# Eight PSUM banks in one pool by stage, second layers behind their twelve Strassen units, two rings of weight loads, and low parts on VectorE

## The chip, the cores and the metric

One core of a Trainium2 chip runs one program. It has five engines with a queue each: TensorE (PE, with weight loads shown apart as PEld), VectorE (DVE), ScalarE (ACT), GpSimd (POOL) and SyncE (SP), which issues the transfers. The metric is the device time of one execution in microseconds, as the median of several runs. Times inside an execution come from one profiled execution.

## The reference

Attention with positive features, then a gated layer. 8 batches, 8 heads, 576 tokens, 64 channels per head, 128 features; then 4608 tokens of 512 channels through a hidden width of 1536.

```
proj = x @ w_phi ; proj -= max(|proj|) per token           # for q and for k
phi  = concat(exp(proj), exp(-proj))                       # 256 features
kv, z = sum_s phi(k) v, sum_s phi(k)
attn = (phi(q) kv) / (phi(q) z + 1e-6)
x    = attn as 4608 x 512
out  = (silu(x @ w_gate) * (x @ w_val)) @ w_out
```

The gate and value weights and the output weights come as 64-bit numbers, which the kernel turns into 32-bit ones itself. Inputs of q and w_phi are scaled up so that the exponents matter.

## The kernel before, in words

Tokens are worked on in chunks of 384 (`CH`), 12 chunks in all, and the hidden width in 12 pieces of 128 (`NFT`), written f. Attention goes by pairs of heads: 32 pairs, four for each batch. To keep 32-bit accuracy with the faster matrix format, an operand is split into a high part and a low part (`hi` by a cast on ACT, `lo` by a subtraction), and a product becomes three matmuls: high by high, high by low, low by high.

The stages are:

1. Pairs 0 to 11 ("early", in plain 32-bit matmuls) give the tokens of the first chunks. Meanwhile `weight_piece` (L303) decodes each 64-bit weight piece by a chain of operations on ACT, DVE and POOL, stores its low part in DRAM (`wlo_dram`), and copies for later (`w32_dram`, `wv_dram`).
2. `first` (L748) makes the hidden tile of a chunk and a piece f: gate and value products into two PSUM banks (`ps_gv`), then a tanh and two products. For chunk 0 the second layer `second` (L807) follows at once, three PSUM banks (`ps_o`) holding the sums of 384 tokens; for chunks 1 to 3 the hidden tiles go to DRAM (`keep`, `h_dram`) and are fetched again (`fetch`, `rest`).
3. `sums` (L844) makes the four weight sums that Strassen's scheme needs, on POOL and ACT.
4. From chunk 4 on, chunks are taken in pairs. `operands` (L912) makes seven operand sums of two chunks' tokens, and `strassen` (L947) makes the gate and value of two chunks for one f with seven products instead of eight: the products of one f are one unit of 42 matmuls of 384 columns. Each product's weights, a variant of 256 KB, are read from `wv_dram`. A unit's sums stand in the two banks of `ps_gv` and in a third one, taken from the three banks of `work`, so two are left to attention. The second layer of chunk c follows a unit behind, cut into three pieces (`piece`) that stand between the next unit's products: nine matmuls of 512 columns, L296. Its low weights come from `wlo_dram`. The hidden tile of chunk c + 1 goes to DRAM, and `rest(c + 1)` does its second layer after the twelve units.

Attention pairs 12 to 31 are "split" (in high and low parts) and run beside stages 2 to 4; chunk pair 4 needs 16 pairs, 6 needs 24, 8 needs 28 and 10 needs 32 of them.

What sets the order: the kernel is written as a list of steps, each with an engine, an assumed cost, what it waits for and a rank. `Plan.run` (L95) goes through assumed time and gives each idle engine its ready step of the lowest rank. The result is a fixed order for each engine, in which the engine then runs; it may not overtake. Where PE has nothing ready in the plan it puts in a filler, a small matmul whose result isn't used (`nothing`, L1100, 128 x 256). Attention on PE has a lower rank number than the products, so it goes first when it is ready; on the other engines the layer's steps go first. The plan gives SP 250 bytes per ns and 2000 ns to land, and POOL 150 + 2.2 n ns.

The loads of variants and of the second layer's low weights go through one ring of 12 slots (`stream`, L899): load n may start when the users of load n - 12 are done. Each load is issued by SP, in order; a load whose slot is not yet free holds what stands behind it.

A few lines that the prediction uses:

```
older = stream_users[n - len(SLOTS_OF)] if n >= len(SLOTS_OF) else x_free[PLAIN - 1]
s5 = add(eng, cost(CH), lambda: on.tensor_tensor(out=hl[b], in0=th(j), in1=hh[b], op=ALU.subtract),
done += [g0, add("POOL", pool2(2 * S), lambda k=k, part=part: nc.gpsimd.tensor_tensor(
    out=flat(ql[k]), in0=flat(part), in1=flat(qh[k]), op=ALU.subtract), [g0, f1], rank)]
```

`hh` and `hl` are the parts of a hidden tile, `qh` and `ql` those of a query's features, `th` a hidden tile, `tb` the operand sums (three of the ring's slots lie in a `tb` tile), `o` the second layer's sums.

Of the kernel before, what the change touches and what calls it, by code (L numbers as in the profile page):

```python
# [54 lines left out]
N_STAGE = 2  # L55


class Step:
    __slots__ = ("eng", "cost", "fn", "left", "then", "rank", "n", "lag", "take", "give", "key", "early")

    def __init__(self, eng, cost, fn, rank, n, lag, take, give, key):
        self.eng, self.cost, self.fn, self.rank, self.n, self.lag = eng, cost, fn, rank, n, lag
        self.take, self.give, self.key = take, give, key
        self.left, self.then, self.early = 0, [], False


class Plan:
# [3 lines left out]
    LAG = {"PE": 220, "ACT": 90, "DVE": 90, "POOL": 90, "SP": 2000}  # L71
    BYTES = 250.0

    def __init__(self, banks, extra):
# [3 lines left out]
        self.extra = list(range(banks, banks + extra))  # L78
        self.banks = banks
        self.bank = {}  # L80
        self.fill = None
        self.early = False

    def add(self, eng, cost, fn, after=(), rank=0.0, take=None, give=None):
        s = Step(eng, cost, fn, rank, len(self.steps), self.LAG[eng], take, give, (rank, len(self.steps)))
        seen = set()
# [5 lines left out]
        s.early = self.early  # L92
# [3 lines left out]
    def run(self):  # L96
        ready = {e: [] for e in self.LAG}
        busy = dict.fromkeys(self.LAG, False)
        for s in self.steps:
# [5 lines left out]
        def start(e):  # L105
# [42 lines left out]
        while events:  # L148
            now = events[0][0]
            while events and events[0][0] <= now:  # L150
                _, _, kind, x = heapq.heappop(events)
                if kind == "free":
                    busy[x] = False
                elif kind == "dep":
# [3 lines left out]
                else:  # L158
                    (self.free if self.bank[x] < self.banks else self.extra).append(self.bank[x])
# [19 lines left out]
def pool2(n):  # L179
    return 150 + 2.2 * n  # L180
# [15 lines left out]
def favor_attention_moe(ctx: ExitStack, tc: tile.TileContext, qT, kT, v, w_phi, wg, wv, wo, out):  # L196
# [40 lines left out]
    th_tiles, hh, hl = sb("th", [P, CH], F32, TH_SETS), sb("hh", [P, CH], F32R, 2), sb("hl", [P, CH], F32R, 2)  # L237
# [51 lines left out]
    plan = Plan(len(work), NT)  # L289
    work += ps_o  # L290
    add = plan.add

# [11 lines left out]
    def weight_piece(f, a, rank):  # L304
# [15 lines left out]
        s1 = add("DVE", dve2(n), lambda: vec.tensor_scalar(  # L320
            out=e, in0=e, scalar1=F64_LEAST, scalar2=F64_MOST, op0=ALU.max, op1=ALU.min), [s0], rank)
        s2 = add("DVE", dve2(n), lambda: vec.tensor_scalar(
            out=eu, in0=eu, scalar1=3, scalar2=0x3FFFFFFF, op0=ALU.logical_shift_left, op1=ALU.bitwise_and), [s1], rank)
        s3 = add("DVE", dve(n), lambda: vec.scalar_tensor_tensor(
            out=xu, in0=high, scalar=0xC0000000, in1=eu, op0=ALU.bitwise_and, op1=ALU.bitwise_or),
            [s2, wa_free[u % len(wa)]], rank)
        s4 = add("DVE", dve2(n), lambda: vec.tensor_scalar(
            out=eu, in0=xu, scalar1=0xFF800000, scalar2=None, op0=ALU.bitwise_and), [s3], rank)
        s5 = add("DVE", dve(n), lambda: vec.scalar_tensor_tensor(  # L329
            out=e, in0=low, scalar=2.0**-52, in1=e, op0=ALU.mult, op1=ALU.mult), [s4], rank)  # L330
        raw_free[u % len(raw)] = s5
        s6 = add("POOL", pool2(n), lambda: nc.gpsimd.tensor_tensor(out=x, in0=x, in1=e, op=ALU.add), [s5], rank)  # L332
        we_free[u % len(we)] = s6
        s7 = add("ACT", act(n), lambda: nc.scalar.copy(hi, x), [s6], rank)
        s8 = add("POOL", pool2(n), lambda: nc.gpsimd.tensor_tensor(out=lo, in0=x, in1=hi, op=ALU.subtract),
                 [s7, *(lo_user[a // 2][f - LOW_SETS[a // 2]] if f >= LOW_SETS[a // 2] else ()), *lo_copied.get(f - LO_SETS, ())], rank)
# [38 lines left out]
    def bring():  # L375
# [10 lines left out]
        for pr in range(NPAIR):  # L386
            hi = add("ACT", act(CH), lambda pr=pr: nc.scalar.copy(xh[0][:, pr], tile()[:, pr]), [load, *x_free[0]], rank)
            lo = add("DVE", dve(CH), lambda pr=pr: nc.vector.tensor_tensor(
# [9 lines left out]
    def attention(i, rank):  # L398
        b, pr = divmod(i, NPAIR)
        early = i < EARLY_PAIRS  # L400
        plan.early = i < BANK_PAIRS
# [18 lines left out]
        v_in = [add("SP", P * 2 * P, lambda h=h: nc.sync.dma_start(vf[:, :, h, :D], vm[:, :, h]),  # L420
# [8 lines left out]
        else:  # L429
            k_hi = add("ACT", act(KW), lambda: nc.scalar.copy(k_parts()[:, 0], kin),  # L430
                       [*k_in, last.get(("khi", i - 1)), *(use("qx") if i == EARLY_PAIRS else ())], rank)
            k_lo = add("DVE", dve(KW), lambda: vec.tensor_tensor(
# [5 lines left out]
        for g, (t0, t1) in enumerate(K_GROUPS):  # L438
# [42 lines left out]
            def values(t0=t0, t1=t1, buf=buf, both=both):  # L481
                for t in range(t0, t1):
                    for s in range(2):
# [9 lines left out]
                     [e1, *v_in, *kv_steps[-1:]], rank, take=None if g else ("kv", i))  # L493
# [662 lines left out]
```

## Time and profile before

| | |
|---|---|
| median of 3 runs | 1370.2 us (1370.13 to 1373.19) |
| the profiled execution | 1368.7 us |
| its span, first to last instruction | 1366.7 us |
| granted clock of PE, mean | 0.981 |
| DMA traffic | 278.37 MB, 204 GB/s |

The page lists busy time by engine, groups of instructions by source line with their mean duration, the idle time before them and what ended it, and the transfers. Further views of the trace are the same by stretches of time, the waits by engine, the chain of work that ended last, and the instructions in order of time. Most of PE's matmuls stand on L296 (a helper), L965 (Strassen's products) and L489 (attention's values).

### The profile page before, as it was taken

The page shows a single profiled execution, that of the slowest core. Times are in us where ns is not written, and L with a number is a line of the kernel's source. Part 1 is how long each engine was busy: PE and PEld are TensorE (multiplying, and loading weights), DVE is VectorE, ACT ScalarE, POOL GpSimd, SP SyncE. Part 2 cuts the span into 40 slices and gives each one's busy share as a digit, 9 for nine tenths or more (in the row PEclk, how much of TensorE's full clock was granted, in tenths as well). Part 3 has the DMA queues.
Part 4 walks back from the last instruction along what each step waited for, and adds up shares of the span by engine and source line. Part 5 has one row for each costly group of instructions (what it writes and reads, how often), then busy time and mean ns, then how long its engine had stood idle before and what let it go on. Part 6 is the DMA issues. An engine that isn't in the chain of part 4 may idle for free. (4 is left out here: it accounts for less than half of the span.)

```text
span 1366.7 us, 20915 instructions
## 1 busy us (share of the span) xinstructions
PE 1264.1 (92%) x7136; PEld 1148.8 (84%) x7136; DVE 919.1 (67%) x1440; ACT 709.4 (52%) x1407; POOL 391.3 (29%) x280
## 2 busy tenths in 40 slices
PE   8999999999979884899899989999989989999998
PEld 7889989999968884778799868898969888788887
DVE  6898679898677787777766696667696533623332
ACT  5777665333556555556555665555665532432333
POOL 1210023444344533334423231223231321201210
PEclk9999999999999996999999999999999999999999
DMA  4643356877666577677766685667674577777774
GB/s 139 198 121 92 93 176 203 254 246 251 204 209 208 186 224 241 193 245 238 236 186 201 202 286 159 194 205 222 197 235 143 192 223 226 243 231 228 221 231 164
DMA packets 203001, 278.37 MB, mean 204 GB/s; under 512 B 61712, under 2 KB 111120, under 8 KB 202896
## 3 DMA queue, kind: packets, MB, share of 16 engines
q1 hardware_dynamic: 202576, 276.91, 64.4%
q8 instruction: 57, 0.93, 0.3%
q14 instruction: 48, 0.39, 0.1%
q10 hardware_dynamic: 320, 0.13, 0.0%
HBM read 206.18 MB, written 70.78 MB: 203 GB/s over the span
## 5 line engine op out<-in xcount | busy, mean ns | idle before, releaser
L296 PE MATMUL o<-w_hi,hl 128*128 128x512 f32 x432 | 174.6, 404 | 14.7 <-DVE hl L801 12.5
L296 PE MATMUL o<-w_hi,hh 128*128 128x512 f32 x432 | 174.0, 403 | 4.2 <-ACT hh L799 2.7
L801 POOL TENSOR_TENSOR hl<-th,hh 128x384 fp32r<-128x384 f32 x48 | 52.5, 1094 | 373.4 <-ACT hh L799 373.3
L296 PE MATMUL gv<-xh,w_big 128*128 128x384 f32 x384 | 134.8, 351 | 10.0 <-DVE th L777 9.7
L799 ACT CAST hh<-th 128x384 fp32r<-128x384 f32 x144 | 73.3, 511 | 131.0 <-DVE th L1029 62.6
L474 ACT ACTIVATE kp<-kp 128x512 f32<-128x512 f32 (+1 forms) x192 | 98.7, 522 | 73.9 <-DVE kp L469 68.7
L296 PE MATMUL gv<-xl,w_big 128*128 128x384 f32 x384 | 130.0, 339 | 0.0
L986 DVE TENSOR_TENSOR th<-th,work 128x384 f32<-128x384 f32 x96 | 52.7, 549 | 106.5 <-ACT th L983 91.2
L983 ACT COPY th<-gv 128x384 f32<-128x384 f32 x144 | 68.6, 478 | 96.5 <-PE gv L965 88.6
L801 DVE TENSOR_TENSOR hl<-th,hh 128x384 fp32r<-128x384 f32 x96 | 74.2, 780 | 65.0 <-ACT hh L799 63.1
L296 PEld LDWEIGHTS o<-w_hi,hl 128*128 128x128 f32 x432 | 82.5, 191 | 40.5 <-DVE hl L801 17.8
L627 POOL TENSOR_TENSOR ql<-qe,qh 128x1152 fp32r<-128x1152 f32 x20 | 56.9, 2844 | 161.7 <-ACT qh L624 152.7
L296 PEld LDWEIGHTS o<-w_hi,hh 128*128 128x128 f32 x432 | 82.7, 192 | 17.9 <-ACT hh L799 4.6
L489 PEld LDWEIGHTS work<-vf,kp 128*128 128x128 f32 x800 | 93.8, 192 | 2.6 <-ACT den L654 1.1
L991 DVE SCALAR_TENSOR_TENSOR th<-th,th 128x384 f32<-128x384 f32 x96 | 69.0, 720 | 38.5 <-ACT th L990 38.2
L489 PE MATMUL work<-vf,kp 128*128 128x65 f32 x800 | 92.9, 273 | 0.9 <-ACT den L654 0.9
L332 POOL TENSOR_TENSOR shared<-shared,shared 128x512 f32<-128x512 f32 x36 | 48.7, 1353 | 156.8 <-DVE shared L329 156.8
L296 PEld LDWEIGHTS gv<-xh,w_big 128*128 128x128 f32 x384 | 73.1, 190 | 15.1 <-DVE th L777 13.4
L990 ACT ACTIVATE th<-th 128x384 f32<-128x384 f32 x96 | 50.3, 524 | 67.0 <-DVE th L986 67.0
L965 PE MATMUL gv<-tb,stream_xh 128*128 128x384 f32 x408 | 82.6, 339 | 2.6 <-DMA stream_xh<-wv_dram 2.5
L965 PE MATMUL gv<-tb,stream_xl 128*128 128x384 f32 x384 | 77.0, 340 | 5.5 <-DMA stream_xl<-wv_dram 5.2
L965 PEld LDWEIGHTS gv<-tb,stream_xh 128*128 128x128 f32 x408 | 71.0, 188 | 7.1 <-DVE th L991 4.0
(172 smaller groups left out, 3321.0 us busy)
## 6 DMA issues: line engine op xcount, KB each, us to landing
tb<-wv_dram SPq DMA_DIRECT2D x92, 256.0 KB, 3.4
stream_xh<-wv_dram SPq DMA_DIRECT2D x84, 256.0 KB, 3.2
stream_xl<-wv_dram SPq DMA_DIRECT2D x80, 256.0 KB, 3.3
stream_w_lo<-wv_dram SPq DMA_DIRECT2D x80, 256.0 KB, 3.4
h_dram<-th SPq DMA_DIRECT2D x84, 192.0 KB, 3.4
th<-h_dram SPq DMA_DIRECT2D x84, 192.0 KB, 3.6
w_lo<-wlo_dram SPq DMA_DIRECT2D x48, 256.0 KB, 3.3
qin<-in_qT_dram SPq DMA_DIRECT2D x32, 288.0 KB, 2.9
```

The costliest lines, as they stand in the source:

```text
L296: nc.tensor.matmul(o, l, r, start=a, stop=z)
L332: s6 = add("POOL", pool2(n), lambda: nc.gpsimd.tensor_tensor(out=x, in0=x, in1=e, op=ALU.add), [s5], rank)
L474: nc.scalar.activation(kpv[:, :m2, s], kpv[:, :m2, 1], AF.Exp, scale=-1.0 if s else 1.0)
L489: nc.tensor.matmul(ps_kv()[:, (2 * s + h) * VD:(2 * s + h + 1) * VD], kp[buf][:, t - t0, h, s], vf[:, t, h], start=t == 0 and h + s == 0, ...
L627: done += [g0, add("POOL", pool2(2 * S), lambda k=k, part=part: nc.gpsimd.tensor_tensor(out=flat(ql[k]), in0=flat(part), in1=flat(qh[k]), ...
L799: s4 = add("ACT", act(CH), lambda: nc.scalar.copy(hh[b], th(j)), [made, hid_free[b]], FIRST)
L801: s5 = add(eng, cost(CH), lambda: on.tensor_tensor(out=hl[b], in0=th(j), in1=hh[b], op=ALU.subtract), [s4], FIRST)
L965: nc.tensor.matmul(o(), l, r, start=begin and k + m == 0, stop=k + m == 3, skip_group_check=True)
L983: return j, add("ACT", act(CH), lambda: nc.scalar.copy(th(j), src()), [*after, th_free[j]], FIRST)
L986: return add("DVE", dve(CH), lambda: vec.tensor_tensor(out=th(j), in0=th(j), in1=src(), op=ALU.add), after, FIRST)
L990: s1 = add("ACT", act(CH), lambda: nc.scalar.activation(th(t), th(j), AF.Tanh, scale=0.5), [ready, th_free[t]], FIRST)
L991: s2 = add("DVE", dve(CH), lambda: vec.scalar_tensor_tensor(out=th(t), in0=th(t), scalar=1.0, in1=th(j), op0=ALU.add, op1=ALU.mult), [s1], ...
```

## The change

All eight banks are one list, `work`, and every use takes a bank by name when its stage begins and gives it back when it ends (`hold`, `let_go`): two for `first`, three for the second layer, four for Strassen. What is left goes to attention. The second layers of both chunks of a pair follow the twelve units, so both chunks' hidden tiles go to DRAM and back, where before only one's did. The variants have a ring of 13 slots, the second layer's low weights one of 6. The low parts of queries (`ql`), the weight chain's sum (`w6`), the low parts of the weight sums (`sl`) and all low parts of hidden tiles are made on DVE; POOL keeps `w8`, `sa` and `h2`. In the plan, steps named `DVE2` (two operands in SBUF, mostly) and POOL steps exclude each other, a transfer takes 2400 ns plus its bytes at 350 per ns, and POOL costs 330 + 2.05 n ns. Hidden tiles that are fetched are split in place, so their ring slot is kept until their second layer is done.

The diff, cut to its core:

```
+ON = {"w6": "DVE2", "w8": "POOL", "ql0": "DVE2", "ql1": "DVE2", "sa": "POOL", "sl": "DVE2", "h2": "POOL"}
...
-    LAG = {"PE": 220, "ACT": 90, "DVE": 90, "POOL": 90, "SP": 2000}
-    BYTES = 250.0
-
-    def __init__(self, banks, extra):
+    LAG = {"PE": 220, "ACT": 90, "DVE": 90, "POOL": 90, "SP": 2400}
+    BYTES = 350.0
+
+    def __init__(self, banks):
...
-                if s.take is not None and not self.free and not (s.early and self.extra):
+                if s.take is not None and not self.free or \
+                        s.port and port["POOL" if e == "DVE" else "DVE"]:
...
-    return 150 + 2.2 * n
+    return 330 + 2.05 * n
...
-    ps_o = [bank(f"o{t}") for t in range(NT)]
-    ps_gv = [bank(f"gv{a}") for a in range(2)]
-    work = [bank(f"work{i}") for i in range(3)]
+    work = [bank(f"work{i}") for i in range(8)]
...
+    def hold(names, after):
+        return {n: add("PE", 1, lambda: None, after, -2.0, take=n) for n in names}
+
+    def let_go(names, after):
+        for n in names:
+            add("PE", 1, lambda: None, after(n), -2.0, give=n)
+
+    ps = lambda name, n=512: work[plan.bank[name]][:, :n]
+
+    def pair_op(on, n, out, in0, in1, op, after, rank):
+        def go():
+            o, a, b = (x() if callable(x) else x for x in (out, in0, in1))
+            (nc.gpsimd if on == "POOL" else nc.vector).tensor_tensor(out=o, in0=a, in1=b, op=op)
+
+        return add(on, (pool2 if on == "POOL" else dve)(n), go, after, rank)
...
-                done += [g0, add("POOL", pool2(2 * S), lambda k=k, part=part: nc.gpsimd.tensor_tensor(
-                    out=flat(ql[k]), in0=flat(part), in1=flat(qh[k]), op=ALU.subtract), [g0, f1], rank)]
+                done += [g0, pair_op(ON["ql" + str(k)], 2 * S, lambda k=k: flat(ql[k]), flat(part), lambda k=k: flat(qh[k]), ALU.subtract, [g0, f1], rank)]
...
-    STREAM = [("xh0", 3), ("xl0", 3), ("w1_lo0", 2), ("w1_lo1", 1), ("w1_big3", 3)]
-    SLOTS_OF = [(tag, i) for tag, n in STREAM for i in range(n)]
-    stream_n, stream_users = [0], {}
+    RINGS = {"w1": [("xh0", 3), ("xl0", 3), ("w1_lo0", 2), ("w1_lo1v", 1), ("w1_big3", 3), ("xh2", 1)],
+             "w2": [("w2_lo2", 1), ("xl2", 3), ("xh2", 2)]}
...
             if f + 1 < NFT:
-                piece(0)
-            piece(1)
+                p2 = prod(f + 1, 1, cb, True, c_free)
             p4 = prod(f, 3, a, False, [s3])
             h1 = add("DVE", dve(CH), lambda t1=t1, a=a: vec.tensor_tensor(out=th(t1), in0=th(t1), in1=a(), op=ALU.mult),
                      [tg1, p4], FIRST)
-            gv_read[f % 2] = h1
-            p3 = prod(f, 2, zb, False, [v2])
-            g2 = plus(j2, zb, [s2, p3])
-            third["free"] = g2
+            a_free[f % 2] = h1
+            keep(c, f, t1, h1)
+            p3 = prod(f, 2, bb, False, [v2])
+            g2 = plus(j2, bb, [s2, p3])
+            b_free = [g2]
...
         t = operands(c)
-        left = strassen(c, t, third, list(waiting))
-        waiting[:] = left
-        rest(c + 1)
-    put_off()
-
-    begun = []
+        before = [ffn["pe"]]
+        ahead = strassen(c, t, hold([("z", n, c) for n in range(4)], before))
+        begin_sums(c, [ffn["pe"]])
+        rest(c, c, ahead)
+        rest(c + 1, c)
+        end_sums(c)
```

Three places show how the order moves. First PE in the last pair of chunks, before: `tb` with a weight slot is a product of a unit (x6: two steps along the contraction, three matmuls each), `o` with `hh` or `hl` a piece of the second layer.

```order
L965 MATMUL gv_140<-tb_4394,stream_xl_4396 128x384 x6
L965 MATMUL gv_139<-tb_4414,stream_xl_4396 128x384 x6
L296 MATMUL o_136<-w_hi_81,hh_127 128x512
L296 MATMUL o_136<-stream_xh_4390,hh_127 128x512
L296 MATMUL o_136<-w_hi_81,hl_129 128x512
L296 MATMUL o_137<-w_hi_81,hh_127 128x512
L296 MATMUL o_137<-stream_xh_4390,hh_127 128x512
L296 MATMUL o_137<-w_hi_81,hl_129 128x512
L965 MATMUL gv_139<-tb_4439,stream_w_lo_4405 128x384 x6
L965 MATMUL work_142<-tb_4439,stream_w_lo_4405 128x384 x6
L296 MATMUL o_138<-w_hi_81,hh_127 128x512
```

And PE in the last pair after the change:

```order
L1019 MATMUL work_138<-tb_4629,stream_xl_4907 128x384 x6
L1019 MATMUL work_132<-tb_4659,stream_xl_4907 128x384 x6
L1019 MATMUL work_137<-tb_4612,stream_w_lo_5072 128x384 x6
L1019 MATMUL work_138<-tb_4659,stream_w_lo_5072 128x384 x6
L1019 MATMUL work_132<-tb_4681,stream_w_lo1v 128x384 x6
L1019 MATMUL work_134<-tb_4612,tb_4681 128x384 x6
L1019 MATMUL work_132<-tb_4629,tb_4681 128x384 x6
L1019 MATMUL work_138<-tb_4629,tb_4681 128x384 x6
```

The pieces of the second layer are gone from between the products, and four banks (132, 134, 137, 138) hold a unit's sums.

The second place is SP's queue at the same time. Before, `stream<-wlo_dram` is the second layer's low weight, in the same slots as the variants from `wv_dram`; `h_dram<-th` stores a hidden tile.

```order
L905 DMA stream_xh_4390<-wv_dram 128x512 x2
L787 DMA h_dram<-th_125 128x384
L905 DMA stream_xl_4396<-wv_dram 128x512
L905 DMA stream_xl_4396<-wlo_dram 128x512
L905 DMA stream_xl_4396<-wv_dram 128x512
L905 DMA stream_w_lo_4405<-wv_dram 128x512 x2
L905 DMA stream_xh_4390<-wv_dram 128x512
```

After the change:

```order
L958 DMA stream_xh_4868<-wv_dram 128x512 x3
L803 DMA h_dram<-m_10523 128x384
L958 DMA stream_xl_4907<-wv_dram 128x512 x3
L958 DMA stream_w_lo_5072<-wv_dram 128x512
L803 DMA h_dram<-m_10503 128x384
L958 DMA stream_w_lo_5072<-wv_dram 128x512
L958 DMA stream_w_lo1v<-wv_dram 128x512
```

No low weight stands among the variants any more, and a unit has two stores of hidden tiles instead of one.

The third place is PE with attention beside a unit, at the numerators of a pair (`qh` and `ql` with `kvh` and `kvl`). Before, in the third pair of chunks:

```order
L965 MATMUL gv_140<-tb_4439,stream_w_lo_4405 128x384 x3
L296 MATMUL work_141<-qh_3064,kvh 128x288
L296 MATMUL work_141<-qh_3064,kvl 128x288
L296 MATMUL work_141<-ql_3065,kvh 128x288
L296 MATMUL work_141<-qh_3066,kvh 128x288
L296 MATMUL work_141<-qh_3066,kvl 128x288
L296 MATMUL work_141<-ql_3067,kvh 128x288
L965 MATMUL gv_140<-tb_4439,stream_w_lo_4405 128x384 x3
```

After the change, in the first pair:

```order
L1019 MATMUL work_132<-tb_4629,stream_w_lo1v 128x384 x6
L315 MATMUL work_135<-qh_3074,kvh 128x288
L315 MATMUL work_135<-qh_3074,kvl 128x288
L315 MATMUL work_135<-ql_3075,kvh 128x288
L315 MATMUL work_135<-qh_3076,kvh 128x288
L315 MATMUL work_135<-qh_3076,kvl 128x288
L315 MATMUL work_135<-ql_3077,kvh 128x288
L315 MATMUL work_138<-qh_3074,kvh 128x288
```

Where one bank took one group of numerators at a time, with products between, groups now follow each other in different banks. On DVE and POOL the moved instructions keep their sizes: 40 of 1152, 48 of 384 and 36 of 512 elements, and 12 of 1024 that become 48 of 256. The fillers on PE are 108 after and 28 before, and 96 more transfers of 384 columns stand on SP.

More of the change, by code (lines that the diff above doesn't have):

```diff
@@ L947, in operands, with strassen @@
         return made
-    def strassen(c, made, third, before):
+    def strassen(c, made, held):
         vec = nc.vector
-        done = {}
         got = {}
+        b_free = [held["z", 0, c]]
+        c_free = [held["z", 1, c]]
+        a_free = [held["z", 2, c], held["z", 3, c]]
         def prod(f, v, o, begin, after=()):
-            if (f, v) not in got:
-                got[f, v] = stream(wv_dram[f, v], wv_stored[f, v])
-            n, load = got[f, v]
+            view, users, load = got[f, v]
             for k in range(2):
                 def go(k=k):
-                    a = stream_view(n)
+                    begun.append(1)
+                    a = view()
                     hi, lo = a[:, k * NF:(k + 1) * NF], a[:, (2 + k) * NF:(3 + k) * NF]
@@ L971, in prod, with fetch_variant @@
                 t_users[v] = [e]
-            done[f, v] = e
             return e
-        gv = lambda f, n: lambda: ps_gv[(f + n) % 2][:, :CH]
-        zb = lambda: work[plan.bank["third"]][:, :CH]
-        b_free = third["free"]
-        pend = before
-        p1 = None
+        def fetch_variant(f, v):
+            if f < NFT:
+                got[f, v] = stream("w1", wv_dram[f, v], wv_stored[f, v])
+        ab = lambda f: lambda: ps(("z", 2 + f % 2, c), CH)
+        bb = lambda: ps(("z", 0, c), CH)
+        cb = lambda: ps(("z", 1, c), CH)
         def copy_out(src, after):
             j = new_th()
-            return j, add("ACT", act(CH), lambda: nc.scalar.copy(th(j), src()), [*after, th_free[j]], FIRST)
+            return j, add("ACT", act(CH), lambda: nc.scalar.copy(th(j), src()), [*after, th_free[j.slot]], FIRST)
         def plus(j, src, after):
@@ L1059, in put_off, with rest, begin_sums, end_sums @@
             waiting.append(job)
+    def rest(c, held, ahead=()):
+        for f in range(NFT):
+            second(c, f, parts(*(ahead[f] if f < len(ahead) else fetch(c, f))), low_parts(f, 1), held)
+    def begin_sums(held, after):
+        names = [("o", t, held) for t in range(NT)]
+        got = hold(names, after)
+        for t, n in enumerate(names):
+            stored[t] = got[n]
+    def end_sums(held):
+        let_go([("o", t, held) for t in range(NT)], lambda name: [stored[name[1]]])
+    begun = []
+    gv_names = lambda held: [("gv", a, held) for a in range(2)]
+    def begin_gv(held, after):
+        got = hold(gv_names(held), after)
+        for a, n in enumerate(gv_names(held)):
+            gv_read[a] = got[n]
+    begin_gv(0, [])
     attend(PLAIN * CH)
+    begin_sums(0, early_done)
     for f in range(NFT):
@@ L1070, in favor_attention_moe @@
             else:
-                put_off(0, f, parts(j, h), low_parts(f, 1, w_ready[f, 2]))
-    def rest(c):
-        for f in range(NFT):
-            put_off(c, f, parts(*fetch(c, f)), low_parts(f, 1))
+                put_off(0, f, parts(j, h), low_parts(f, 1, w_ready[f, 2]), 0)
+    put_off()
+    ffn["ring"] += 2
+    th_free[TH_SETS] = th_free[TH_SETS + 1] = last["nu", EARLY_PAIRS - 1]
     for f in range(NFT):
@@ L1078, in favor_attention_moe @@
     bring()
-    rest(1)
+    rest(1, 0)
     for f in range(NFT):
-        j, h = first(PLAIN - 1, f, low_parts(f, 0))
+        j, h = first(PLAIN - 1, f, low_parts(f, 0), 0)
         keep(PLAIN - 1, f, j, h)
-    rest(2)
-    rest(PLAIN - 1)
-    third = {"free": add("PE", 1, lambda: None, x_free[PLAIN - 1], -2.0, take="third")}
-    ffn["ring"] += len(TH_TAGS)
-    ring_on.append(1)
+    let_go(gv_names(0), lambda name: [gv_read[name[1]]])
+    rest(2, 0)
+    rest(PLAIN - 1, 0)
+    end_sums(0)
+    ffn["ring"] += 2
+    ring_on.append(len(lo_user[1]))
+    paced.extend(lo_user[1][-NFT:])
     for j in range(2):
```

308 lines of the change are left out of this document (173 added, 135 removed).

## The prediction

> **What bounds the kernel now.** I read the head of the page first, then busy time by stage, then the waits of TensorE (PE) stage by stage, then the chain of waits in the last stage.
>
> ```profile
> PE 1264.1 (92%) x7136; PEld 1148.8 (84%) x7136; DVE 919.1 (67%) x1440; ACT 709.4 (52%) x1407; POOL 391.3 (29%) x280
> ...
> 0.00:350.00 350.00, 336.67 (x1990) 310.33 (x1991) 291.51 (x496) 195.57 (x425) 94.68 (x81) 1.00 0.57 178
> 350.00:600.00 250.00, 210.44 (x1180) 188.34 (x1178) 181.52 (x253) 137.95 (x256) 99.41 (x62) 0.92 0.66 210
> 600.00:1100.00 500.00, 469.16 (x2733) 428.06 (x2732) 352.14 (x534) 291.37 (x563) 154.54 (x97) 1.00 0.67 209
> 1100.00:1366.70 266.70, 247.82 (x1240) 222.09 (x1238) 93.89 (x159) 84.50 (x166) 42.63 (x40) 0.99 0.70 222
> ```
>
> PE is busy for 1264.1 of 1366.7 us and no other engine is near it, so the time can fall only by what PE loses. In the windows the first figure is the stretch, then the busy time of PE, PEld, DVE, ACT and POOL, then the granted clock, the DMA share and GB/s. PE's idle time is 13.3, 39.6, 30.8 and 18.9 us: 102.6 in all. In the second stage the clock is 0.92 as well, which costs up to 0.08 x 250 = 20 us more. The change takes no matmul of the computation away, so about 120 us is all there is to win.
>
> ```profile
> PE work L296 <- ACT qx L587: 15.8, 2, 14.6
> PE o L296 <- DVE hl L801: 6.8, 4, 4.0
> PE gv L296 <- DVE th L777: 6.2, 3, 3.6
> PE work L296 <- DVE kp L469: 5.1, 4, 2.7
> ...
> 536.26 0.61 PE L296 MATMUL work<-qh,kvh 128*128 128x288 f32 x1 [14.59 <-ACT qx L587]
> ...
> 516.19 2.98 POOL L627 TENSOR_TENSOR ql<-qe,qh 128x1152 fp32r<-128x1152 f32 x1 [14.63 <-ACT qh L624]
> ...
> 516.66 3.20 DVE L432 TENSOR_TENSOR ks<-kin,ks 128x640 fp32r<-128x640 f32 x1
> ```
>
> These are waits of 350 to 600 us (total, times, longest), and one place in it. VectorE (DVE) and GpSimd (POOL) both work between SBUF tiles there, and the DVE operation ends just after the POOL operation that began before it: 3.20 us for 640 elements, where 1152 elements take 1.35 (row L611 below). So DVE falls behind the order in which the program was written, ACT and attention follow it, and PE, which may not overtake, stands still for 14.59 us.
>
> ```profile
> 1251.36 1.40 PE o L296 x6
> ...
> 1253.82 1.04 PE work L965 x6
> 1254.86 0.48 PE o L296 x2
> ...
> 1255.35 3.62 DMA stream_xh<-wv_dram
> ...
> 1259.11 2.32 PE gv L965 x12
> 1261.43 1.40 PE o L296 x6
> ...
> 1322.42 1.40 PE o L296 x6
> ...
> 1190.65 23.36 PE o L296 x99
> ```
>
> This is the chain in the last pair of chunks. It goes from the last piece of a second layer (o) to a load of a weight variant (wv_dram) and back to PE, unit after unit. From 1251.36 to 1322.42 seven units pass, 10.15 us each. Six variant products take 1.04 us, so seven groups of six matmuls take 7.3; nine of the second layer's take 9 x 23.36/99 = 2.12. PE's own work is 9.4 us, and 0.75 is lost per unit. The reason is in the queue: the low weights of the second layer share the ring of 12 slots with the variants. Their slot is free only when the next unit's last piece is done, and SyncE, which is in order, holds all later loads behind the one that wants it.
>
> **The change, part by part.**
>
> Ring split (stage from 1100 us). The 831 matmuls of the variants in that stage are 19.8 units:
>
> ```profile
> 1100.00:1366.70 266.70, 158.26 (x831) 147.00 (x831) 0.99 0.70 222
> ```
>
> 19.8 x 0.75 is 15 us of that stage's 18.9 idle. With a ring of their own the variants are loaded in the order of use, 13 ahead, 13/7 of a unit or 13.5 us, against loads that land in 3 to 4 us. I take **-15**. What is late next is bandwidth. A unit without its second layer moves 7 x 0.262 + 2 x 0.197 = 2.23 MB (both chunks' hidden tiles are now stored) in 7.3 us, 305 GB/s.
>
> ```profile
> 1214.00:1336.00 122.00, 116.59 (x616) 107.87 (x614) 39.56 (x72) 37.88 (x76) 23.39 (x23) 1.00 0.76 234
> 1330.00:1340.00 10.00, 9.85 (x45) 7.82 (x45) 3.25 (x6) 4.70 (x10) 2.28 (x2) 1.00 0.95 324
> ```
>
> Before, such a stretch ran at 234 GB/s with a share of 0.76, and 324 with 0.95 has been reached. The 13 slots are full when a pair begins (3.4 MB), so twelve units need (26.7 - 3.4) MB in 87 us: 268 GB/s. I take **+3** for the four pairs; from 0 to +25 (third rival). The Trainium skill, "DMA: Bandwidth & Descriptors", section Bandwidth, gives 138 GB/s for a 64 KB transfer and 341 for 1 MB and asks for 1 MB pieces; halfway, 240 GB/s as an estimate from that page, two pairs without attention would lose 20 us and the sum would be 1330. The row with 324, made of pieces of 192 and 256 KB, speaks against it.
>
> Second layers behind the units. 96 more transfers of 192 KB go through SyncE, whose issues lie beside PE. What is on the path is the turn from units to second layers: only two hidden tiles are fetched ahead, for 2 x 2.12 us.
>
> ```profile
> th<-h_dram SPq DMA_DIRECT2D x84, 192.0 KB, 3.6
> ...
> L801 DVE TENSOR_TENSOR hl<-th,hh 128x384 fp32r<-128x384 f32 x96 | 74.2, 780 | 65.0 <-ACT hh L799 63.1 <-DMA th<-h_dram 1.5 <-issue 0.2
> ```
>
> The third needs 3.6 us to land, a cast and 0.78: about 1 us late, four times: **+4** (0 to +12, if three such waits follow each other). The reverse turn waits for no load, since 24 second layers give 50 us to refill.
>
> POOL to DVE. Moved are 40 operations of 1152 elements, 48 of 384, 36 of 512, and 12 of 1024 (as 48 of 256).
>
> ```profile
> L627 POOL TENSOR_TENSOR ql<-qe,qh 128x1152 fp32r<-128x1152 f32 x20 | 56.9, 2844 | 161.7 <-ACT qh L624 152.7 <-DVE kp L469 9.0
> L611 DVE TENSOR_TENSOR qx<-qx,qe 128x1152 f32<-128x1152 f32 x20 | 27.0, 1350 | 0.7
> L986 DVE TENSOR_TENSOR th<-th,gv 128x384 f32<-128x384 f32 x48 | 26.5, 551 | 12.4 <-PE gv L965 12.3
> L329 DVE SCALAR_TENSOR_TENSOR shared<-shared,shared 128x512 f32<-128x512 uint32 x36 | 24.9, 691 | 1.1
> L515 DVE TENSOR_TENSOR kvl<-work,kvh 128x256 fp32r<-128x256 f32 x40 | 16.6, 416 | 12.8 <-ACT kvh L511 12.6
> L801 POOL TENSOR_TENSOR hl<-th,hh 128x384 fp32r<-128x384 f32 x48 | 52.5, 1094 | 373.4 <-ACT hh L799 373.3
> L332 POOL TENSOR_TENSOR shared<-shared,shared 128x512 f32<-128x512 f32 x36 | 48.7, 1353 | 156.8 <-DVE shared L329 156.8
> L866 POOL TENSOR_TENSOR s<-s,shi 128x1024 fp32r<-128x1024 f32 x12 | 28.8, 2403 | 30.8 <-ACT shi L865 30.8
> ```
>
> DVE gains 40 x 1.350 + 48 x 0.551 + 36 x 0.691 + 48 x 0.416 = 125 us. From POOL go 40 x 2.84 + 52.5 + 48.7 + 28.8 = 244 of its 391 us. That is also time in which POOL can hold DVE: hl took 780 ns against 551 for the same size read from PSUM, 22 us in 96 operations. The new rules also keep POOL and such DVE operations apart. DVE's cover is its idle time, 68 us in stage two and 148 in stage three. I count the added 125 us at nothing on the path (second rival if the cover fails), and the waits as follows. The 14.59 us stall goes, with it most of the 50 us around it, 500 to 550:
>
> ```profile
> 500.00:550.00 50.00, 31.71 (x167) 28.52 (x167) 39.05 (x48) 25.43 (x44) 14.48 (x8) 0.76 0.66 214
> ```
>
> 18.3 us idle and 0.24 x 50 = 12 us of clock: **-30** (0 to -30). Of the other DVE waits in stage two (6.8 + 6.2 + 5.1) two thirds, because nearly that share of POOL's work goes: **-12**. The Trainium skill, "SBUF — State Buffer", section Who interferes with whom, says that a VectorE instruction with two SBUF inputs and a GpSimd instruction that reads SBUF shut each other out for the whole instruction. The 3.20 us row agrees; by the rule the 147 us that stay on POOL can still block, so a third of the waits is kept in either case.
>
> Stage three, with four or five banks for attention where it had two:
>
> ```profile
> PE gv L965 <- DMA tb<-wv_dram: 5.7, 2, 3.4
> PE o L296 <- DVE hl L801: 5.7, 5, 1.7
> PE work L965 <- DVE th L986: 4.7, 4, 1.7
> PE work L296 <- DVE kp L469: 3.2, 3, 1.4
> PE gv L965 <- DMA stream_xl<-wv_dram: 2.0, 2, 1.2
> ```
>
> Two thirds of the DVE waits (13.6) and of the loads (7.7): **-14**. Banks have no row of their own; if they alone set the attention waits the rest of 30.8 goes too (first rival), if not nothing more.
>
> Fillers. The matmuls that only keep PE occupied rise from 28 to 108, because the plan sees more waits.
>
> ```profile
> L1102 PE MATMUL gv<-wbd_hi 64*128 64x256 f32 x23 | 4.1, 337 | 6.6 <-ACT wbd_hi L280 6.6
> ```
>
> 80 x 4.1/23 = 14 us if all stand in the way, 0 if PE would have waited: **+7**. Stage one stays: its 13.3 us are mostly the start (6.6), and the weight path there gives 36 POOL operations of 1.35 us for 36 of 0.69 on DVE.
>
> Sum: 1366.7 - 15 + 3 + 4 - 30 - 12 - 14 + 7 = 1309.7 of span. The profiled execution was 1368.7 us, 2.0 outside the span; the median is 1370.2, 1.5 over that. With 3.5 on top: 1313.
>
> **Rivals.**
>
> First, more goes than I count: all idle time after 350 us is 89.3 us, the clock 20; if nine tenths of that go, 98 us, and +7 of fillers come, the time is 1370.2 - 98 + 7 = 1279. For it speaks that most waits have one root, DVE held by POOL; against it that PE's waits in stage three have four kinds of releaser.
>
> Second, **slower**: DVE becomes the bound while attention runs, 350 to 1000 us. It is at 73% and 70% there and takes most of the 125 us. If two thirds of these delay attention, and PE behind it, the time is 1313 + 83 = 1396. It decides against the change from 57 us on, 46% exposed. Against it: 216 us of idle time in two stages, and POOL's holds that end.
>
> Third, the units become bound by DMA. At the 234 GB/s of before, (26.7 - 3.4)/0.234 = 100 us instead of 87 for each of two pairs without attention: +25, so 1338.
>
> Fourth, the stalls only move: the ring's part comes (-15), and the 56 us of stages two and three return at other places of the new order: 1369. That the change does not do what it says is excluded by the rows of the order.
>
> **How the numbers follow.** Forecast 1313, chance 0.58 (own range 1290 to 1340, from the ends of stall, turn and fillers); first rival 0.17; third 0.08; fourth 0.07; second 0.10. Faster by over 0.3% (4 us, about what a measurement of this kernel tells from no change): 0.58 + 0.17 + 0.08 and a fifth of the fourth, 0.84. Within: 0.04. Slower: 0.12, the second and a share of the fourth. The range goes from 1272, just under the first rival, to 1360, and leaves out the second, most of the fourth and the tail below.
>
> **What would show it.** Right: in attention-free pairs units 7.3 to 7.6 us apart and DMA near 290 GB/s; no PE wait over 10 us near the first unit; the ks operation near 0.8 us; hl near 0.55; POOL near 145 us, DVE 950 to 1040; PE idle of 50 to 70 us. Wrong: units over 8 us with loads as releasers (third), PE waits on DVE with DVE over 85% (second), PE idle near 100 us elsewhere (fourth).

## The result, and the profile after

| | before | after |
|---|---|---|
| median of 3 runs | 1370.2 us (1370.13 to 1373.19) | 1295.2 us (1293.81 to 1295.84) |
| ratio, 95% interval | | 0.9444 [0.9421, 0.9467] |
| span of the profiled execution | 1366.7 us | 1294.0 us |
| granted clock of PE, mean | 0.981 | 0.993 |

The kernel is 75 us faster; the prediction said 57 (1313, range 1272 to 1360). First the head of the page after and busy time by stretches. The units begin earlier now, so the stretches are cut where the last stage of attention and the last two pairs lie; columns as before.

```profile
PE 1250.9 (97%) x7216; PEld 1155.5 (89%) x7216; DVE 938.4 (73%) x1612; ACT 708.4 (55%) x1419; POOL 150.8 (12%) x144
...
0.00:350.00 350.00, 333.59 (x1960) 306.30 (x1961) 294.82 (x524) 195.44 (x423) 47.84 (x46) 1.00 0.57 176
350.00:550.00 200.00, 186.77 (x1065) 170.03 (x1064) 160.46 (x273) 115.22 (x217) 48.50 (x50) 0.97 0.79 256
550.00:930.00 380.00, 374.79 (x2365) 356.03 (x2364) 318.08 (x535) 260.80 (x512) 23.69 (x21) 1.00 0.75 237
930.00:1294.00 364.00, 355.76 (x1832) 323.11 (x1830) 165.07 (x283) 136.98 (x269) 30.74 (x27) 1.00 0.80 259
```

PE's idle time is 16.4, 13.2, 5.2 and 8.2 us: 43.1 where it was 102.6. That is 59.5 of the 72.7 us by which the span fell. The other 13.2 are in the busy time itself, 1264.1 to 1250.9, although 80 fillers came: the same matmuls took less time on the record, with the clock at 0.993 for 0.981. VectorE, with 172 operations more than before, is at 84% in the third stretch (318.08 of 380), and PE waits for it 0.8 us there, 10.1 us in the whole execution. These are PE's waits (total, times, longest); the first five rows are of the whole execution, the last two of 600 to 1294 us alone:

```profile
PE work L315 <- DMA w_lo<-wlo_dram: 9.6, 5, 4.4
PE work L1182 <- ACT wbd_hi L284: 6.8, 1, 6.8
PE work L1019 <- ACT m L1038: 6.6, 7, 2.2
PE work L315 <- DVE m L793: 4.7, 7, 1.1
PE work L315 <- DMA qin<-in_qT_dram: 3.3, 2, 1.7
...
PE work L1019 <- ACT m L1038: 6.6, 7, 2.2
PE work L315 <- ACT qx L604: 1.6, 2, 0.8
```

The longest is the start of the program (L1182). Behind 600 us PE waits 9.0 us in all, and 6.6 of them are for the copy of a unit's sums out of their bank (m, L1038), mostly in a pair's last unit.

The chain of waits of after, from 1150 us on, is nearly one engine; before it had a load of a variant in most units:

```profile
1149.90 1.39 PE work L315 x6
1151.29 85.60 PE work L1019 x492
1236.89 0.02 issue
1236.91 0.49 ACT m L1038
1237.40 0.04 issue
1237.44 2.36 PE work L1019 x12
1239.80 50.32 PE work L315 x216
```

These are the last pair's 504 products (twelve units of 42), 88.5 us in all, and then the 216 matmuls of two second layers. The units start 7.28 us apart. In the stretch that holds only units PE has no idle time at all, and the transfers run at 302 GB/s:

```profile
1170.00:1230.00 60.00, 60.00 (x348) 59.91 (x347) 25.91 (x49) 20.29 (x42) 9.03 (x9) 1.00 0.92 302
```

VectorE's operations between SBUF tiles are shorter. These groups of after (busy, mean ns) answer to rows of 780 ns (hl, now m<-m,hh) and to two that were not shown:

```profile
L308 DVE TENSOR_TENSOR m<-m,hh 128x384 fp32r<-128x384 f32 x132 | 75.0, 573 | 91.9 <-ACT hh L818 88.0 <-DMA stream_xl<-wlo_dram 3.1 <-DMA m<-h_dram 0.5
L591 DVE TENSOR_TENSOR qs<-qin,qs 64x576 fp32r<-64x576 f32 x40 | 34.7, 868 | 3.1 <-ACT qs L589 2.1
L449 DVE TENSOR_TENSOR ks<-kin,ks 128x640 fp32r<-128x640 f32 x20 | 16.9, 844 | 0.3
```

Of before:

```profile
L574 DVE TENSOR_TENSOR qs<-qin,qs 64x576 fp32r<-64x576 f32 x40 | 53.0, 1324 | 6.5 <-ACT qs L572 5.6
L432 DVE TENSOR_TENSOR ks<-kin,ks 128x640 fp32r<-128x640 f32 x20 | 32.3, 1613 | 5.6 <-ACT ks L430 5.3
```

So VectorE, which was given 125 us of work by the forecast's count, is busy only 19 us longer.

### The profile page after: what moved, and what is told of

It is laid out like the page before. It is cut to its first block, busy times and chain, and to the rows that moved or that the text cites. A ratio compares the mean times of both kernels' runs of the same rounds, so it can differ in the third digit from the quotient of the medians.

```text
span 1294.0 us, 21402 instructions
## 1 busy us (share of the span) xinstructions
PE 1250.9 (97%) x7216; PEld 1155.5 (89%) x7216; DVE 938.4 (73%) x1612; ACT 708.4 (55%) x1419; POOL 150.8 (12%) x144
## 4 chain that ended last, share of the span: by engine, by line
PE 78%; DMA 9%; DVE 8%; ACT 2%; SPq 1%; issue 1%; ACTq 0%; DVEq 0%
PE work L315 43%; PE work L1019 25%; PE work L506 8%; DMA w_lo<-wlo_dram 3%; DMA h_dram<-m 2%; DMA m<-h_dram 1%; PE work L502 1%; DMA qin<-in_qT_dram 1%; DVE shared L341 1%; PE work L569 1%; DVE shared L348 1%; DVE shared L343 1%; PE work L1184 1%; DVE shared L308 1%; DVE m L796 0%
## 5 line engine op out<-in xcount | busy, mean ns | idle before, releaser
L315 PE MATMUL work<-w_hi,hh 128*128 128x512 f32 x468 | 183.1, 400 | 0.4 <-DVE m L1041 0.4
L315 PE MATMUL work<-w_hi,m 128*128 128x512 f32 x396 | 157.8, 398 | 0.0
L1041 DVE TENSOR_TENSOR m<-m,work 128x384 f32<-128x384 f32 x144 | 78.2, 551 | 100.2 <-ACT m L1038 73.0
L315 PE MATMUL work<-xh,w_big 128*128 128x384 f32 x384 | 135.2, 352 | 5.3 <-DVE m L793 4.7
L315 PE MATMUL work<-xl,w_big 128*128 128x384 f32 x384 | 129.7, 338 | 0.0
L1019 PE MATMUL work<-tb,stream_xh 128*128 128x384 f32 x618 | 114.7, 336 | 2.6 <-ACT m L1038 2.2
L1038 ACT COPY m<-work 128x384 f32<-128x384 f32 x144 | 68.9, 479 | 85.7 <-PE work L1019 74.5
L1019 PEld LDWEIGHTS work<-tb,stream_xh 128*128 128x128 f32 x618 | 107.0, 188 | 3.6 <-ACT m L1038 2.6
L315 PEld LDWEIGHTS work<-w_hi,hh 128*128 128x128 f32 x468 | 88.5, 189 | 20.5 <-DVE m L1041 0.6
L1019 PE MATMUL work<-tb,stream_xl 128*128 128x384 f32 x468 | 90.1, 340 | 1.7 <-ACT m L1038 1.7
L1019 PEld LDWEIGHTS work<-tb,stream_xl 128*128 128x128 f32 x468 | 82.5, 191 | 2.2 <-ACT m L1038 2.1
```

Source lines behind the costliest of these rows:

```text
L315: nc.tensor.matmul(o, l, r, start=a, stop=z)
L1019: nc.tensor.matmul(o(), l, r, start=begin and k + m == 0, stop=k + m == 3, skip_group_check=True)
L1038: return j, add("ACT", act(CH), lambda: nc.scalar.copy(th(j), src()), [*after, th_free[j.slot]], FIRST)
L1041: return add("DVE", dve(CH), lambda: vec.tensor_tensor(out=th(j), in0=th(j), in1=src(), op=ALU.add), after, FIRST)
```

## The experiments

Twelve kernels, each compared with the kernel before on the same chip (its median there was 1370 to 1373 us). Behind each time stand its ratio to the kernel before and the 95% interval of that ratio. A difference between two changed kernels goes across chips, so 2 or 3 us of it mean nothing. Where an edit gives a step another engine or cost, the plan orders all steps anew: such a run prices the edit together with the order that it brings.

### The moved work: queries' low parts on GpSimd or VectorE

**On the changed kernel, moved back.**

```
-ON = {..., "ql0": "DVE2", "ql1": "DVE2", ...}
+ON = {..., "ql0": "POOL", "ql1": "POOL", ...}
```

> The changed kernel with the low parts of queries back on GpSimd (40 operations of 1152 elements); the plan still keeps GpSimd and two-operand VectorE steps apart. Theory (where these 40 stand matters, since each holds VectorE for nearly 3 us): 1305 to 1320 us, PE idle time up by 10 us or more between 350 and 930 us, VectorE waits on the path. Rival (the plan's knowledge of the exclusion is enough, wherever they stand): 1291 to 1299 us.

Measured 1320.3 us, 0.962 [0.9574, 0.9667]: 25 us of the gain go (the plan also put in 24 more fillers). Most of it lies between the first units of the second and the third pair, 210 us apart where the changed kernel has 191. VectorE's qs operation is at 1126 ns again:

```profile
L591 DVE TENSOR_TENSOR qs<-qin,qs 64x576 fp32r<-64x576 f32 x40 | 45.0, 1126 | 22.6 <-ACT qs L589 21.7
```

**On the kernel before, this move alone.**

```
-done += [g0, add("POOL", pool2(2 * S), ... nc.gpsimd.tensor_tensor(
+done += [g0, add("DVE", dve(2 * S), ... vec.tensor_tensor(
```

> The kernel before with one part of the change alone: the low parts of the queries' exponentials (two operations per pair from the split pairs on) go from GpSimd to VectorE; plan, banks, turns and ring as before. On the changed kernel, putting them back on GpSimd cost 25 us. Theory A, the move is worth the same by itself, since it takes a 2.98 us GpSimd operation off the chain and frees VectorE of waits on the port: 1340-1350, with GpSimd near 145 us busy and VectorE's mean time of the paired operations down. Theory B, it needs the banks and the order of the rest: within 1362-1372.

Measured 1334.6 us, 0.9726 [0.9708, 0.9745]: 38 us from 40 moved operations, more than theory A said. (GpSimd fell to 275.6 us and not to 145: the other low parts stay on it here, which the expectation overlooked.) The qs and ks operations, which the edit does not touch, fell as on the changed kernel:

```profile
L574 DVE TENSOR_TENSOR qs<-qin,qs 64x576 fp32r<-64x576 f32 x40 | 33.1, 828 | 5.9 <-ACT qs L572 5.0
L432 DVE TENSOR_TENSOR ks<-kin,ks 128x640 fp32r<-128x640 f32 x20 | 20.3, 1015 | 2.9 <-ACT ks L430 2.4 <-DMA stream_w_lo<-wv_dram 0.4
```

But the stretch in which the 14.59 us stall lay is not mended. 500 to 550 us of this kernel, the two longest waits in it, and VectorE just ahead of them:

```profile
500.00:550.00 50.00, 33.93 (x172) 29.74 (x171) 41.06 (x56) 28.51 (x48) 11.78 (x10) 0.80 0.73 239
...
533.60 0.58 PE L296 MATMUL work<-wbd_hi,ks 128*128 128x256 f32 x1 [4.74 <-DVE kvl L515]
542.09 0.48 PE L296 MATMUL work<-wst_hi,ks 128*128 128x128 f32 x1 [6.84 <-DVE kp L469]
...
522.64 1.83 DVE L926 TENSOR_TENSOR tb<-stage,tb 128x768 fp32r<-128x768 f32 x2
...
526.59 1.82 DVE L926 TENSOR_TENSOR tb<-stage,tb 128x768 fp32r<-128x768 f32 x2
528.45 0.96 DVE L931 TENSOR_TENSOR stage<-stage,stage 128x768 f32<-128x768 f32 x1
```

From 522.64 to 533.2 us VectorE makes the operand sums of the first pair: eleven operations of 0.95 us with only two others between them. They stand ahead of attention by rank. The wait of 4.74 us is for a `kvl` that stands behind them, the one of 6.84 us for a `kp` that stands behind them and another 7 us of attention's own work on VectorE; the two are there in place of 14.59. The same eleven stood there before, and beside GpSimd's operations they took 16 us:

```profile
520.90 2.98 DVE L926 TENSOR_TENSOR tb<-stage,tb 128x768 fp32r<-128x768 f32 x1
...
534.97 1.93 DVE L926 TENSOR_TENSOR tb<-stage,tb 128x768 fp32r<-128x768 f32 x2
536.82 0.77 DVE L592 STREAM_TRANSPOSE qe<-qx 128x576 f32<-128x576 f32 x1
```

ScalarE casts for these sums in its own fixed order, and the copy `qx` for which PE waited 14.59 us stands behind those casts:

```profile
533.34 0.83 ACT L925 CAST tb<-stage 128x768 fp32r<-128x768 f32 x1 [2.79 <-DVE stage L931]
...
534.61 0.38 ACT L587 COPY qx<-work 128x288 f32<-128x288 f32 x1
```

The changed kernel makes them from 522.46 to 536.8 us, but among low parts of hidden tiles, on which PE can work meanwhile:

```profile
500.00:550.00 50.00, 45.77 (x237) 39.90 (x236) 40.98 (x69) 27.17 (x53) 8.27 (x8) 0.97 0.78 248
...
527.27 0.94 DVE L979 TENSOR_TENSOR tb<-stage,tb 128x768 fp32r<-128x768 f32 x1
528.37 1.03 DVE L308 TENSOR_TENSOR m<-m,hh 128x384 fp32r<-128x384 f32 x2 [0.16 <-ACT hh L818]
529.32 0.95 DVE L984 TENSOR_TENSOR stage<-stage,stage 128x768 f32<-128x768 f32 x1
530.52 0.56 DVE L308 TENSOR_TENSOR m<-m,hh 128x384 fp32r<-128x384 f32 x1 [0.25 <-ACT hh L818]
```

And with the queries' low parts back on GpSimd (the experiment above) it still has no stall there:

```profile
500.00:550.00 50.00, 45.87 (x242) 38.44 (x241) 43.20 (x69) 29.02 (x54) 8.61 (x6) 0.97 0.71 223
```

So this stretch was mended by the rest of the change, not by the move. It was not the plan's numbers either: with all the old ones on the changed kernel (below) PE is busy for 46.60 of these 50 us at a clock of 0.95, and under the new plan the kernel before has 40.05 at 0.76. Nor was it the banks that attention gets (with few of them 48.78 at 0.96) or the ring (with the move 34.16 at 0.83). That leaves the other low parts on VectorE and the new order of the second layers and their banks, which were not tried by themselves. What the move pays lies elsewhere: the four pairs of the kernel before began their units at 629, 840, 1046 and 1214 us, with the move alone at 625, 819, 1016 and 1182.

### The ring split

**On the kernel before, alone:** a ring of 7 slots for the second layer's low weights, the variants keep their 12.

```
-m, load = stream(wlo_dram[f, :, 2 * DM:], [lo_stored[f, 2]])
+m, load = low_stream(wlo_dram[f, :, 2 * DM:], [lo_stored[f, 2]])
...
```

> The kernel before, with one part of the change alone: the low weights of the second layer get a ring of their own (7 slots), the variants keep their 12; second layers still stand between the products. Theory (the shared ring costs 0.75 us per unit): 1348 to 1356 us, units of the last pair 9.4 to 9.6 us apart where they were 10.15. Rival (another wait takes its place, bandwidth or the products' own chain): 1364 to 1372 us, units still 10 us apart.

Measured 1361.5 us, 0.9922 [0.9895, 0.9949]. Where no attention is left, the units of the last two pairs start 9.43 us apart where the last pair had 10.15, as was forecast: from the third pair's first unit to the fourth's 154 us pass where 168 did, and from there to the end 146 where 153 did. That is 21 us, but 14 of them are given back: the third pair began at 1060 us instead of 1046. Ahead of it PE lost clock in one place and idle time and clock in another.

```profile
480.00:560.00 80.00, 58.93 (x313) 53.59 (x312) 59.64 (x73) 42.54 (x76) 24.26 (x14) 0.79 0.66 210
620.00:700.00 80.00, 67.50 (x354) 60.69 (x354) 51.14 (x72) 43.35 (x83) 30.44 (x21) 0.85 0.62 195
```

The kernel before has 58.69 us and 0.83 in the first stretch, 73.41 us and 1.00 in the second; what was added in the second is a wait for `qx` (4.8 us for 0.8), and its cause was not followed up. This edit also raises the slots from 12 to 19. Whether one shared ring of 19 slots would do as well was not tried, so the shared use is shown as the cause only as far as its size and place fit.

**Both parts together on the kernel before.** The two edits above.

> The kernel before with two parts of the change and nothing else: the low parts of the queries' exponentials on VectorE (alone: 1334.6 us against 1372.6, so 38 us) and the second layer's low weights in a ring of their own (alone: 1361.5 against 1372.1, so 10.6 us, with units of the last two pairs 9.43 us apart instead of 10.15). Theory A, the two parts work at different places, so they add: 1322-1328. Theory B, the ring's 14 us in the last two pairs come through whole here, because the stall near the first unit, which moved with it before, is gone: 1315-1321. Theory C, the time that the ring gains is given back again earlier: 1330-1337. What is left to the 1295.2 us of the changed kernel then belongs to the turns behind the units, the banks and the plan's transfer numbers together.

Measured 1306.3 us, 0.9531 [0.9494, 0.9567]: 65 us, below every theory's range. Alone the parts gave 38 and 11. The units are 9.43 us apart and the pairs begin at 621, 812, 1003 and 1158 us, so against the move alone 18 of the 31 us of span come behind the third pair's start, where the ring was priced, and 13 ahead of it; nothing is given back now.

```profile
350.00:600.00 250.00, 217.75 (x1237) 195.37 (x1236) 188.78 (x282) 149.64 (x277) 61.97 (x53) 0.93 0.72 228
600.00:1100.00 500.00, 495.18 (x2929) 466.16 (x2929) 354.89 (x578) 295.70 (x573) 86.47 (x75) 1.00 0.74 228
```

Behind 600 us this kernel idles as little as the changed one. Ahead of it 32.3 us of idle time and a clock of 0.93 are left, the waits of 4.74 and 6.68 us behind the operand sums among them. All the rest of the change (banks, second layers behind the units, the other low parts, plan, fillers) is worth the 11 us from 1306.3 to 1295.2, beside these two parts; in 350 to 600 us it has 13.6 us of idle time for these 32.3.

### The plan's numbers

**Old costs, no exclusion of POOL and VectorE**, on the changed kernel:

```
-"SP": 2400 ... BYTES = 350.0 ... 330 + 2.05 * n
+"SP": 2000 ... BYTES = 250.0 ... 150 + 2.2 * n
-        s.port and port["POOL" if e == "DVE" else "DVE"]:
```

> The changed kernel ordered by the plan of before: no exclusion of GpSimd and VectorE, GpSimd at 150 + 2.2 n ns, transfers at 250 bytes per ns plus 2000 ns. Theory (the stalls of before came from an order made without the exclusion, so most of the gain in stages two and three needs the new plan): 1315 to 1340 us, with PE waits on VectorE of over 15 us in all. Rival (the moved instructions, banks and rings carry the gain, the plan's numbers little): 1295 to 1303 us.

Measured 1326.1 us, 0.9666 [0.9638, 0.9693]. The next two split this.

**Only the exclusion taken out:**

> The changed kernel, ordered by a plan that lets GpSimd and two-operand VectorE steps overlap; GpSimd's and the transfers' new costs stay. Theory (the exclusion in the plan carries most of the 27 us that the old plan cost): 1308 to 1322 us. Rival (with 150 us of GpSimd work left the exclusion hardly matters, and the transfers' numbers carried it): 1294 to 1300 us.

Measured 1300.0 us, 0.9489 [0.9455, 0.9524]: 5 us, not clear of the noise, since the interval overlaps that of the change ([0.9421, 0.9467]). Its theory fell. GpSimd has only 150 us of work left that could collide; that this is the reason is argued.

**Only the transfers' numbers old** (2000 ns, 250 bytes per ns):

> The changed kernel, with transfers planned at 250 bytes per ns plus 2000 ns as before; exclusion and GpSimd's costs stay. If the exclusion carries the plan's share: 1295 to 1303 us, with units of the last pair at 7.3 us. If the transfers' numbers do: 1308 to 1325 us, with units of the last pair at 7.8 us as with the old plan.

Measured 1327.1 us, 0.9709 [0.9659, 0.9758]: the whole loss. Units of the last two pairs are 7.8 us apart instead of 7.28, with two waits of some 0.24 us in each for a product on VectorE. The first begins at 624 us instead of 598, and the plan put in 249 fillers instead of 108:

```profile
1207.43 1.33 PE L1019 MATMUL work<-tb,stream_w_lo1v 128*128 128x384 f32 x6 [0.24 <-DVE m L1041]
...
L1184 PE MATMUL work<-wbd_hi 64*128 64x256 f32 x227 | 32.0, 288 | 0.0
...
L1184 PE MATMUL work<-wbd_hi 64*128 64x256 f32 x88 | 14.1, 295 | 0.0
```

(The first two rows are of this kernel, the third of the changed one; the other 22 and 20 fillers stand on L1182.)

The old numbers cost this much only in company. The kernel before with the move and the ring split is ordered by the old numbers too, and takes 1306.3 us, 20 us less than the 1326.1 of the changed kernel under the old plan. So banks, second layers behind the units and the other low parts lose time together unless the plan's numbers are new as well.

**The same without the filler product:**

```
 def nothing():
+    return
```

> The plan with the old transfer numbers (250 bytes per ns, 2000 ns) placed 249 fillers on TensorE where the changed kernel has 108, and took 1327.1 us against 1295.2. This kernel is that one with the filler product left out of the program (the plan's order is otherwise kept). Theory A, the old numbers cost by fillers that stand where no wait was: the 141 added ones, at some 0.12 to 0.15 us of TensorE's time each, are 17 to 21 us, and the time falls to 1305-1312 with the first unit of Strassen starting 10 us or more earlier than at 624 us. Theory B, the fillers stand where TensorE waits anyway and the order itself costs: 1322-1330, with more idle time of TensorE in 0-624 us in place of the fillers' busy time.

Measured 1313.1 us, 0.9566 [0.9543, 0.959]: some 14 of the 32 us were fillers that stood where PE need not have waited. The other 18 are the order: units are still 7.8 us apart and the first starts at 612. The time falls between the two theories.

**Faster transfers still in the plan**, 420 bytes per ns:

> The changed kernel with its plan told that transfers move 420 bytes per ns in place of 350 (latency 2400 ns kept); the plan then places 71 fillers in place of 108. Theory A, what the plan believes of transfers acts as a smooth knob, and faster is better until loads are really late: 1288-1294, with fewer fillers and waits on loads of TensorE no more than 15 us in all. Theory B, 350 is already near what the transfers reach (slices up to 312 GB/s), and a plan that believes more puts products ahead of their data: 1297-1310, with waits on the low weights above 15 us.

Measured 1302.1 us, 0.9483 [0.9464, 0.9502]: 7 us slower than the change, theory B's time without its reason, since PE's waits on low weights are 10.8 us:

```profile
PE work L315 <- DMA w_lo<-wlo_dram: 6.7, 7, 2.2
...
PE work L315 <- DMA w_lo1g<-wlo_dram: 4.1, 2, 3.1
```

The units keep their 7.28 us; the loss is ahead of the second pair (829 us for 816). Which step of the order causes it wasn't followed up.

**The new plan on the kernel before** (costs and exclusion, nothing moved):

> The kernel before, ordered by the new plan alone (exclusion, GpSimd at 330 + 2.05 n ns, transfers at 350 bytes per ns plus 2400 ns); no instruction moves to another engine, banks and rings stay. Theory (the order's ignorance made the 14.6 us stall, but 391 us on GpSimd still shut VectorE out): 1335 to 1358 us, no TensorE wait above 8 us. Rival (the plan alone gives nothing without the moved work): 1365 to 1385 us.

Measured 1385.4 us, 1.0108 [1.0073, 1.0143], 1% slower than before, where the theory had 1335 to 1358. PE does not idle more (91.3 us for 102.6), and the waits for VectorE are no longer than the 9.7 and 12.5 us that the same two rows had before. But PE is busy for 24 us more, with 82 more fillers and a clock of 0.970 for 0.981:

```profile
PE 1288.2 (93%) x7218; PEld 1176.8 (85%) x7218; DVE 900.8 (65%) x1440; ACT 712.3 (52%) x1407; POOL 384.7 (28%) x280
...
PE gv L305 <- DVE th L786: 9.3, 10, 1.9
PE o L305 <- DVE hl L810: 8.4, 10, 1.6
```

The exclusion and two costs change at once here; which of them does it was not tried.

### Banks and fillers

**Few banks** on the changed kernel: attention from pair 8 on gets at most three banks, two once units run, as before.

```
+late = (take[0] in "kqnt" or take[0] == "kv") and take[1] >= BANK_PAIRS
+return late and self.mine >= (2 if self.units else 3)
...
```

> The changed kernel with attention from pair 8 on held to three PSUM banks, and to two from the first Strassen unit on, as before the change; all else the same. Theory (banks alone set little): 1295 to 1303 us. Rival (two banks were what made attention wait in stage three, and the part of the gain beyond the forecast is theirs): 1312 us or more, PE idle in 550 to 930 us up from 5 to over 20 us.

Measured 1299.3 us, 0.9459 [0.9425, 0.9493]: 4 us, not clear of the noise (its runs go from 1295.0 to 1304.4). PE idles for 6.0 us in 600 to 1100 us, so the rival's over 20 did not come.

**No fillers** on the changed kernel (the edit shown above):

> The changed kernel without the 108 matmuls that only keep TensorE occupied; the plan and all else are the same. By the forecast's term they cost 7 us (0 to 14): 1281 to 1295 us. Rival (they stand where TensorE would wait anyway, or the granted clock falls without them): 1295 to 1305 us.

Measured 1295.4 us, 0.9448 [0.9419, 0.9477]: no difference. Without them PE waits longer for the same things (the low weights 13.9 us for 9.6) and the clock is 0.985.

No kernel tried was faster than the changed one.

## Why the prediction was right, and where not

The sum had seven terms, -71 of gain and +14 of cost. The 75 us measured are a little more than the whole gain and nothing of the cost. The time lies as near to the first rival's 1279 as to 1313, and the 18 us between forecast and result are terms that were mis-sized, the costs above all.

- **What bounds it** held: PE alone, and what it loses by idle time and clock. 59.5 us of the 72.7 came from idle time.
- **Ring split, -15.** Its mechanism and its place were shown by the units: 10.15 to 9.43 us on the kernel before, 7.28 without the second layers between. Its worth hangs on company: 11 us alone, 28 with the move. The step missed that the loads' gain behind 1000 us is only cashed if nothing ahead becomes late. Why the two parts together bring 65 us, where 38 and 11 add up to 49, is not shown beyond this.
- **Bandwidth, +3 (0 to 25).** Measured zero: no unit of the last two pairs waits for a load, at 302 GB/s. The estimate of 240 GB/s from the Trainium skill, "DMA: Bandwidth & Descriptors", section Bandwidth, and its sum of 1330 are not borne out here, with many pieces of 192 and 256 KB in flight.
- **Turn to second layers, +4 (0 to 12).** Zero: at all four turns (740, 954, 1100 and 1240 us) PE goes from the products to the second layers without a gap, as the chain shows for the last one. ScalarE, which casts a fetched tile first, did wait for fetches, 33.4 us in 27 times over the whole execution, but not so long that PE ran out of tiles.
- **Stall and clock at 500 to 550 us, -30.** The size was nearly right: idle 18.3 to 4.2 us, clock 0.76 to 0.97, so some 24 us. That was luck, since the cause was wrong by half. The row of 3.20 us agrees with GpSimd's hold, but behind it stood the operand sums, 16 us of VectorE, which the prediction did not look at. With the move alone the stretch lost almost as much (33.93 us busy, 0.80); with the rest of the change and the old place of the queries' low parts, no more than the changed kernel.
- **Two thirds of other waits, -12 and -14.** In stage two, idle time outside 500 to 550 us fell from 21.3 to 9.4, 12 us as forecast. Stage three was mis-sized: in 600 to 1100 us it fell from 30.8 to 8.6, 22 us for 14 (the units begin 31 us earlier, so the work in the stretch is not quite the same). The one root, VectorE slowed by GpSimd, had been seen, and it reached further than the waits that name VectorE: 40 qs and 20 ks operations alone took 85.3 us before and 51.6 after. This is the reason of the first rival. Its size was not reached: of the 89.3 us of idle time behind 350 us 62.7 went, seven tenths for its nine.

```profile
600.00:1100.00 500.00, 491.39 (x2960) 467.25 (x2959) 372.24 (x626) 300.35 (x590) 40.34 (x35) 1.00 0.79 251
```

- **Fillers, +7 (0 to 14).** Zero by the run without them. They can cost, some 14 us for 141 more, where the plan thinks loads slower than they are.
- **Banks, no row of their own.** Nothing that stands clear of the noise, as counted.
- **The second rival**, VectorE as the bound, fell though VectorE reached 84%. **The third**, units bound by DMA, fell by the 7.28 us. **The fourth**, stalls that only move, happened where one part stood alone (the ring's 14 us, the operand sums), not in the whole.
- Of the signs named, ks (0.84 us), hl (0.57), GpSimd (150.8), and waits under 10 us near the first unit came as said; PE's idle time (43 us for 50 to 70) and VectorE (938 for 950 to 1040) came out lower. The plan's numbers got no term in the prediction. The changed kernel loses 32 us without the new numbers for transfers, though the two parts on the kernel before reach 1306.3 us without them: the order was read from the rows, but not asked what it rested on.

## What to carry to other kernels

Price a GpSimd operation by what it does to VectorE's operations between SBUF tiles, too: compare the same operation's mean on both sides of it, and count every operation that shrinks, not only the waits that name it. When a stall has a cause in the trace, look at what stands next in that engine's queue before counting the stall as gone. And in an order that a plan fixes ahead, the assumed speed of transfers is part of the kernel: measure it, and try it on both sides.

## What had not been expected of the hardware

- A low clock stood where PE idled. Before, 500 to 550 us had PE busy for 31.71 of 50 us at a clock of 0.76, the changed kernel 45.77 at 0.97; with the ring alone 58.93 of 80 us went with 0.79 and 67.50 of 80 with 0.85. So in these places a stall of PE went with a second loss; which of them brings the other wasn't tried.
- On the changed kernel, pieces of 256 KB (landing in 3.6 to 4.0 us) and 192 KB reached 302 GB/s over 60 us, with a DMA share of 0.92, and PE did not wait.
- 40 operations less on GpSimd made the kernel before 38 us faster though VectorE took them all, and VectorE's whole busy time fell, from 919.1 to 914.7 us.
